# Token-wise convolution with expert routing: gate scores of two groups through the convolution, one softmax buffer, 128-row weight loads

## The chip, the cores and the metric

The kernel runs on one core of one Trainium2 chip. The metric is device time in microseconds (us) of one execution; three runs of the kernel before gave 272.96, 272.98 and 274.2 us, median 272.98.

## What is computed

```
w   = exp(weight_gen - max);  w = w / (sum over the 7 taps + 1e-9)        # (8, 4160, 8, 7)
out = einsum('bshk,bskhg->bshg', w, x_unf)     # x_unf: the token and the 6 before it, 8 heads x 24
...
scores  = einsum('bsd,d->bs', out, w_gate)                                # one score per token
for b in range(8):
    top_idx = argpartition(-scores[b], 128)[:128]
    xe = out[b, top_idx]
    ye = maximum(xe @ w1, 0) @ w2                                         # 192 -> 1024 -> 192
    out[b, top_idx] = xe + sigmoid(scores[b, top_idx])[:, None] * ye
```

x and weight_gen have 8 batches of 4160 tokens, in fp32. Every token has its own softmax weights over seven taps for each of 8 heads of 24 columns; then 128 tokens of each batch go through a small expert network.

## The kernel before, in words

**Tiling.** The 33280 tokens are cut into 278 windows of W = 120 tokens; a window takes 128 partitions (6 earlier tokens ahead of it). Four windows make a unit (U = 4), so there are 70 units, 0 to 69. The weights are handled in three groups of windows, GROUPS = ((0,80),(80,176),(176,278)), which are units 0 to 19, 20 to 43 and 44 to 69.

**Softmax.** Each group's weights are loaded in five chunks (`load_w`, 80, 96 or 102 rows of 5376 bytes) and handled with a window on a partition: `sm_exp` on ScalarE (L225), the sum over taps `sm_den` (VectorE L279 in group 0, GpSimd L283, L284, L287 in the others), the reciprocal as a logarithm and an exponential on ScalarE (L295, L297), `sm_start` (L267) and the product `sm_norm` (L309) on VectorE. The result stands in one of two buffers `amem`; `wt_head` transposes it on TensorE to `wt`, a token on a partition.

**Convolution.** Step si of a hand-written schedule does one piece of each of several units. GpSimd casts a unit of x to fp16 (`cast_x`, L164). VectorE multiplies wt with a mask (`band`, L766) into banded 128 x 128 matrices, one for each window and head: 128 x 3840 elements for a unit. For units in PBS, 50 to 65, one of the four windows is made on GpSimd, and VectorE's piece is 128 x 2880. `conv` is 32 matmuls (L792) with a band as weights and 24 columns of x. ScalarE copies the PSUM result (`evac`, L814) and SP stores it.

**Scores.** The score of a token is a sum over taps and heads of its softmax weight times the dot of an x row's head with the gate. The dots: `y_t` transposes x of a unit (L358, six matmuls), `y_x` copies xT out of PSUM (L369 on ScalarE, L367 on VectorE for every fifth unit), `y_d` (L381, L384, L387) multiplies it with the gate matrix gmat, and `y_e` (L392) keeps the dots in y16. When a group's dots are whole, `score_t` transposes them (L407), `score_x` copies them twice (Y0 and the same shifted by a token, L418, L419), `score_p` multiplies the softmax weights with them (L435, four pieces of 1920 elements), `score_m` sums over heads on TensorE (L451, four times eight matmuls), `score_r` adds the taps (L463) and `score_s`, `score_l` carry the scores through DRAM into the layout of the selection.

**Selection and experts.** After the last scores, candidates (L544 to L547), ranks (L588, L593, L600) and index lists (L606 to L628) follow on VectorE and TensorE. GpSimd then gathers 128 rows of each batch (`ex_gather`, L705), TensorE runs the two layers (L717, L730, L732, L740), VectorE adds (L742), and GpSimd scatters the rows back (`ex_scatter`, L747).

**What sets the order.** Each engine works through its own queue in the order in which the program issues. A step issues, in this order: moves due first (`pre`), loads and casts (`feed`), the band of unit si + 2, the copy and the store of unit si - 1, xT copies, moves due at its head (`first`), the convolution of unit si, the dots and transposes of later units, and the rest of its planned moves (`plan`):

```
        if si + 2 < NS and si >= 1:
            band(si + 2)
        if 1 <= si <= NS:
            evac(si - 1)
...
        if si < NS:
            conv(si)
        for j, u in enumerate(yd[si]):
            y_d(u, cts[si], j)
        for u in yt[si]:
            y_t(u)
        for mv in plan[si]:
            mv()
```

With Y_END = 47 the last dots are kept in step 49, where the scores of group 2 begin (`sc_moves`).

Of the kernel before, what the change touches and what calls it, by code (L numbers as in the profile page):

```python
# [18 lines left out]
P = 128  # L19
# [15 lines left out]
NV = 5  # L35

# [62 lines left out]
def fast_path(  # L99
# [11 lines left out]
    wrp = ctx.enter_context(tc.tile_pool(name="wrp", bufs=3))  # L111
# [3 lines left out]
    dtp = ctx.enter_context(tc.tile_pool(name="dtp", bufs=1))  # L115
    spp = ctx.enter_context(tc.tile_pool(name="spp", bufs=2))
# [9 lines left out]
    ps_m = ctx.enter_context(tc.tile_pool(name="ps_m", bufs=1, space=bass.MemoryType.PSUM))  # L126

# [62 lines left out]
    def load_w(gi, ci, home=None):  # L190
# [23 lines left out]
    def a_view(gi):  # L214
        return amem[gi % 2][:, 0:M * H * Q * 8].rearrange("p (c q k) -> p c q k", c=M * H, q=Q)
# [5 lines left out]

    def sm_exp(gi, ci):
        n, q0, q1, nq, col, cq = dims(gi, ci)
        wr = wraws.pop((gi, ci))
        nc.scalar.activation(  # L225
# [3 lines left out]
        )  # L229

# [72 lines left out]
    def sm_norm(gi, ci):  # L303
        n, q0, q1, nq, col, cq = dims(gi, ci)
        r2 = sm.pop((gi, ci))
        if gi and SE:
            sm_start(gi, ci, nc.vector)
        v = a_view(gi)[0:n, :, q0:q1, :].rearrange("p c q (k b) -> p c q k b", b=2)
        nc.vector.tensor_tensor(  # L309
# [3 lines left out]
        )  # L313
# [5 lines left out]
    def wt_t(gi, h):  # L319
# [4 lines left out]
        am = amem[gi % 2]  # L324
        tp = ps_t.tile([P, M, P], FP16, tag="tps", name="wtps")
# [22 lines left out]
    y16 = ypl.tile([P, NU * U, H], FP16, name="y16")  # L348
    ystate = {}

    def ntr(u):
        return nwin(u) * D // P

    def y_t(u):
        xf = xs[u].rearrange("p t d -> p (t d)")
        tp = ps_t.tile([P, M, P], FP16, tag="tps", name="xtps")
        for r in range(ntr(u)):
            nc.tensor.transpose(  # L358
                out=tp[:, r, :], in_=xf[:, r * P:(r + 1) * P], identity=ident16[:, :]
            )  # L360
        ystate[u] = tp

    def y_x(u, eng):
        tp = ystate.pop(u)
        xT = xtp.tile([P, NT, P], FP16, tag="xT", name="xT")
        if eng == "v":
            nc.vector.tensor_copy(out=xT[:, 0:ntr(u), :], in_=tp[:, 0:ntr(u), :])  # L367
        else:
            nc.scalar.copy(out=xT[:, 0:ntr(u), :], in_=tp[:, 0:ntr(u), :])  # L369
        ystate[u] = xT  # L370

    def y_d(u, cps, j):

        xT = ystate.pop(u)
        o = 2 * D + j * U * H
        yps = cps[:, 0, o:o + U * H].rearrange("p (w h) -> p w h", h=H)
        for r in range(ntr(u)):
            q, w = divmod(r, 3)
            lhs = xT[:, r, :]
            if w == 0:  # L380
                nc.tensor.matmul(out=yps[:, 2 * q, :], lhsT=lhs, rhs=gmat[:, 0, :],  # L381
                                 start=True, stop=False, skip_group_check=True)
            elif w == 1:
                nc.tensor.matmul(out=yps[:, 2 * q:2 * q + 2, :], lhsT=lhs, rhs=gmat[:, 1:3, :],  # L384
                                 start=False, stop=False, skip_group_check=True)
            else:
                nc.tensor.matmul(out=yps[:, 2 * q + 1, :], lhsT=lhs, rhs=gmat[:, 3, :],  # L387
                                 start=False, stop=True, skip_group_check=True)

    def y_e(us, cps):  # L390
        n = sum(nwin(u) for u in us)
        nc.scalar.copy(  # L392
            out=y16[:, us[0] * U:us[0] * U + n, :],
            in_=cps[:, 0, 2 * D:2 * D + n * H].rearrange("p (w h) -> p w h", h=H),
        )
# [890 lines left out]
```

## Time and profile before

| | |
|---|---|
| median of three runs | 272.98 us |
| the profiled execution's own time | 273.41 us |
| its span in the profile | 271.7 us |
| VectorE (DVE) busy | 225.9 us, 83% |
| TensorE (PE) / ScalarE (ACT) / GpSimd (POOL) busy | 169.4 / 169.6 / 163.5 us |
| moved by DMA | 63.74 MB |

The span runs from the first to the last recorded instruction; 273.41 - 271.7 = 1.7 us lie around it. The tables by stretch cut the span where the first band is made (28.4 us), where the last transposes of the dots start (178.3), where the scores are back from DRAM (199.6) and where the first gather can start (228.3). Busy time is that of instructions on an engine; a DMA share near 1 means that all 16 DMA engines had work nearly all the time.

### The profile page before, as it was taken

The page shows a single profiled execution, that of the slowest core. Times are in us where ns is not written, and L with a number is a line of the kernel's source. Part 1 is how long each engine was busy: PE and PEld are TensorE (multiplying, and loading weights), DVE is VectorE, ACT ScalarE, POOL GpSimd, SP SyncE. Part 2 cuts the span into 40 slices and gives each one's busy share as a digit, 9 for nine tenths or more (in the row PEclk, how much of TensorE's full clock was granted, in tenths as well). Part 3 has the DMA queues.
Part 4 walks back from the last instruction along what each step waited for, and adds up shares of the span by engine and source line. Part 5 has one row for each costly group of instructions (what it writes and reads, how often), then busy time and mean ns, then how long its engine had stood idle before and what let it go on. Part 6 is the DMA issues. An engine that isn't in the chain of part 4 may idle for free.

```text
span 271.7 us, 8756 instructions
## 1 busy us (share of the span) xinstructions
PE 169.4 (62%) x3605; PEld 157.1 (58%) x3605; DVE 225.9 (83%) x247; ACT 169.6 (62%) x331; POOL 163.5 (60%) x207
## 2 busy tenths in 40 slices
PE   0006577666787899466879697774833145499950
PEld 0006566656786899456778597774822134498740
DVE  4898999989999994998999868989989998495100
ACT  4763586889889367698797669561233922268620
POOL 8876596877337438989653623398346904863421
PEclk9999985556999656675589869655555555559965
DMA  7999999999999999989999969859446230746410
GB/s 173 248 296 271 272 274 253 292 312 317 345 343 324 309 316 330 320 260 326 340 352 358 353 180 251 281 161 203 89 116 189 62 109 17 234 127 185 131 45 22
DMA packets 77528, 63.74 MB, mean 235 GB/s; under 512 B 6488, under 2 KB 75648, under 8 KB 77483
## 3 DMA queue, kind: packets, MB, share of 16 engines
q1 hardware_dynamic: 75002, 60.76, 75.8%
q0 software_dynamic: 2032, 2.36, 3.9%
q8 instruction: 30, 0.49, 0.7%
q14 instruction: 16, 0.12, 0.1%
q10 hardware_dynamic: 448, 0.00, 0.1%
HBM read 37.41 MB, written 26.49 MB: 235 GB/s over the span
## 4 chain that ended last, share of the span: by engine, by line
DVE 29%; DMA 19%; issue 15%; PE 13%; POOL 12%; ACT 8%; SPq 1%; POOLq 1%; DVEq 0%; ACTq 0%
DMA xst<-in_x_dram 9%; DMA wraw<-in_weight_gen_dram 5%; DVE band__161 L766 5%; PE sps L451 4%; DVE band__162 L766 4%; ACT amem L225 3%; DVE band__163 L766 3%; DMA out_dram<-co 3%; DVE junk L593 3%; POOL s L283 3%; DVE amem L309 2%; DVE den L279 2%; PE cps L792 2%; POOL out_dram L747 2%; DVE sp L435 2%
## 5 line engine op out<-in xcount | busy, mean ns | idle before, releaser
L164 POOL CAST x<-xst 128x768 f16<-128x768 f32 x70 | 61.1, 887 | 46.4 <-DMA xst<-in_x_dram 30.5
L814 ACT COPY co<-cps 128x768 f32<-128x768 f32 x70 | 55.5, 797 | 32.4 <-PE cps L387 13.8
L358 PE MATMUL xtps<-ident,x 128*128 128x128 f16 x417 | 43.4, 268 | 11.6 <-DVE xT L367 6.1
L766 DVE TENSOR_TENSOR band__161<-wt,mask 128x3840 f16<-128x3840 f16 (+2 forms) x24 | 47.9, 1994 | 0.6 <-PE cps L792 0.5
L766 DVE TENSOR_TENSOR band__163<-wt,mask 128x3840 f16<-128x3840 f16 (+1 forms) x23 | 46.3, 2012 | 1.7 <-ACT wt L341 1.2
L766 DVE TENSOR_TENSOR band__162<-wt,mask 128x3840 f16<-128x3840 f16 (+1 forms) x23 | 46.8, 2033 | 0.2 <-PE cps L792 0.2
L369 ACT COPY xT<-xtps 128x768 f16<-128x768 f16 (+1 forms) x56 | 44.1, 817 | 2.2 <-PE xtps L358 2.2
L358 PEld LDWEIGHTS <-x 128*128 128x128 f16 x417 | 33.2, 121 | 12.8 <-POOL x L164 8.5
L792 PE MATMUL cps<-x,band__161 128*128 128x24 f16 x752 | 24.0, 179 | 10.4 <-DVE band__161 L766 8.9
L792 PEld LDWEIGHTS <-band__161 128*128 128x128 f16 x752 | 23.5, 103 | 11.5 <-DVE band__161 L766 9.5
L792 PEld LDWEIGHTS <-band__163 128*128 128x128 f16 x736 | 22.9, 102 | 9.5 <-issue 8.1
L792 PE MATMUL cps<-x,band__163 128*128 128x24 f16 x736 | 23.2, 178 | 8.1 <-ACT co L814 4.2
L792 PE MATMUL cps<-x,band__162 128*128 128x24 f16 x736 | 23.6, 179 | 3.5 <-DVE band__162 L766 2.2
L328 PE MATMUL wtps<-ident,amem 80*128 80x80 f16 (+2 forms) x192 | 13.1, 233 | 19.8 <-DVE amem L309 17.6
L792 PEld LDWEIGHTS <-band__162 128*128 128x128 f16 x736 | 22.9, 103 | 4.1 <-DVE band__162 L766 2.4
L451 PE MATMUL sps<-sp,ident 80*80 80x240 f16 (+2 forms) x96 | 18.1, 362 | 9.8 <-DVE sp L435 5.0
L328 PEld LDWEIGHTS <-amem 80*128 80x128 f16 (+2 forms) x192 | 11.6, 117 | 20.8 <-DVE amem L309 17.7
L381 PE MATMUL cps<-gmat,xT 128*128 128x8 f16 x139 | 15.5, 168 | 12.1 <-DVE xT L367 11.8
L225 ACT ACTIVATE amem<-wraw 96x1344 f16<-96x1344 f32 (+2 forms) x13 | 17.2, 1320 | 7.4 <-DVE sp L435 3.6
L451 PEld LDWEIGHTS <-ident 80*80 80x80 f16 (+2 forms) x96 | 15.4, 172 | 10.4 <-issue 6.7
L309 DVE TENSOR_TENSOR amem<-amem,r 80x1536 f16<-80x1536 f16 (+2 forms) x15 | 19.0, 1267 | 0.7 <-ACT r L297 0.2
L381 PEld LDWEIGHTS <-xT 128*128 128x128 f16 x139 | 11.9, 100 | 12.7 <-DVE xT L367 12.4
(177 smaller groups left out, 387.9 us busy)
## 6 DMA issues: line engine op xcount, KB each, us to landing
xst<-in_x_dram SPq DMA_DIRECT2D x68, 384.0 KB
out_dram<-co SPq DMA_DIRECT2D x69, 360.0 KB
wraw<-in_weight_gen_dram SPq DMA_DIRECT2D x10, 504.0 KB
wraw<-in_weight_gen_dram SPq DMA_DIRECT2D x3, 420.0 KB
amem<-in_weight_gen_dram SPq DMA_DIRECT2D x2, 420.0 KB
wea<-in_moe_w_dram POOLq DMA_DIRECT2D x1, 384.0 KB, 8.0
xst<-in_x_dram SPq DMA_DIRECT2D x1, 288.0 KB
wea<-in_moe_w_dram POOLq DMA_DIRECT2D x1, 256.0 KB, 6.7
```

Of the source, the lines that this page charges most:

```text
L164: nc.gpsimd.tensor_copy(out=t.rearrange("p u d -> p (u d)")[:, 0:n], in_=xst.pop(u).rearrange("p u d -> p (u d)")[:, 0:n],)
L225: nc.scalar.activation(out=a_view(gi)[0:n, :, q0:q1, 0:K].rearrange("p c q k -> p q c k"), in_=wr[0:n, 0:nq * M, :].rearrange("p (q m) (h ...
L283: nc.gpsimd.tensor_tensor(out=s4, in0=av[:, :, :, 0:4], in1=av[:, :, :, 4:8], op=ALU.add)
L309: nc.vector.tensor_tensor(out=v, in0=v, in1=r2[0:n, 0:cq, :].rearrange("p (c q) b -> p c q b", q=nq)[:, :, :, None, :] .to_broadcast([n, M ...
L328: nc.tensor.transpose(out=tp[:, m, 0:n], in_=am[0:n, o:o + P], identity=ident16[0:n, 0:n])
L358: nc.tensor.transpose(out=tp[:, r, :], in_=xf[:, r * P:(r + 1) * P], identity=ident16[:, :])
L369: nc.scalar.copy(out=xT[:, 0:ntr(u), :], in_=tp[:, 0:ntr(u), :])
L381: nc.tensor.matmul(out=yps[:, 2 * q, :], lhsT=lhs, rhs=gmat[:, 0, :], start=True, stop=False, skip_group_check=True)
L451: nc.tensor.matmul(out=sps[0:n].rearrange("p m q k -> p m (q k)"), lhsT=ident16[0:n, 0:n], rhs=sp[0:n, :, h, :], start=(h == 0), stop=(h = ...
L766: eng.tensor_tensor(out=bt[:, o:o + n * H * BC].rearrange("p (c q m) -> p c q m", q=NQ, m=M), in0=wts[gi][:, l:l + n].rearrange("p w h m - ...
L792: nc.tensor.matmul(out=cps[:, w // 2, (w % 2) * D + h * G:(w % 2) * D + (h + 1) * G], lhsT=bt[:, o:o + P], rhs=xwin(si * U + w)[:, h * G:( ...
L814: nc.scalar.copy(out=co.rearrange("p (j w) d -> p j (w d)", w=2)[:, 0:n], in_=cts[si][:, 0:n, 0:2 * D],)
```

## The change

- **Scores of groups 0 and 1 by the convolution.** A head of x becomes 25 columns (GY = 25) instead of 24: the cast writes runs of 24 into rows of 25, and `y_k` (ScalarE) puts the head's dot into the 25th. For units below 44 `conv` runs with 25 columns, so a score per head stands beside the result; `y_s` (ScalarE) copies it in fp32 for every step, and at a group's end `head_m` (eight fp32 matmuls against the identity) sums over heads and transposes, `head_x` copies and stores. `score_t`, `score_x`, `score_p`, `score_m` and `score_r` are gone for these two groups.
- **Transposes.** A unit of x has 800 columns now, seven transposes, xT of 896 columns. The gate matrix is built from a row by matmuls and selects (`gate_mats`). The dots of the first four units are made ahead of the loop (YP = 4); Y_END is 50, the last dots are kept in step 52.
- **Group 2** reads the transposed dots out of PSUM directly (no copies; the shifted ones come from a transpose with a turned identity); its four `score_p` stand in one step, its four sums in the next.
- **One softmax buffer.** `amem` is single, group 2's softmax moves from steps after group 0's scores to 17 to 32 (SM2), its transposes to 33 to 40 (WT2). One clearing of the second buffer (L866) is gone, and of group 0's sums over taps one goes to TensorE (seven matmuls).
- **Weight loads.** `wrp` has five buffers instead of three. Chunks of groups 0 and 1 are loaded with 128 rows instead of 80 and 96; all five of group 1 are issued ahead of the loop.
- **GpSimd** makes a quarter of the band for units 52 to 61 instead of 50 to 65. The order of gathers and scatters at the end differs.

The diff, cut:

```diff
+GY = G + 1
+DY = H * GY
-    wrp = ctx.enter_context(tc.tile_pool(name="wrp", bufs=3))
+    wrp = ctx.enter_context(tc.tile_pool(name="wrp", bufs=5))
...
+        if u < XR:
+            nc.gpsimd.memset(t[:, :, G], 0.0)
         nc.gpsimd.tensor_copy(
-            out=t.rearrange("p u d -> p (u d)")[:, 0:n],
-            in_=xst.pop(u).rearrange("p u d -> p (u d)")[:, 0:n],
+            out=t[:, 0:n, 0:G],
+            in_=xst.pop(u).rearrange("p u (h g) -> p (u h) g", g=G)[:, 0:n],
         )
...
-        cuts = [0, n // 16 * 16] + ([n] if n % 16 else [])
+        if n > 60 and w0 + P < TOT:
+            cuts = [0, P]
+        else:
+            cuts = [0, n // 16 * 16] + ([n] if n % 16 else [])
...
+    def y_k(u, yps):
+        n = nwin(u) * H
+        nc.scalar.copy(out=xs[u][:, 0:n, G], in_=yps.rearrange("p w h -> p (w h)")[:, 0:n])
...
+    def y_s(si):
...
+            nc.scalar.copy(
+                out=ysc[:, si * U:si * U + n, :].rearrange("p (j w) h -> p j (w h)", w=2),
+                in_=cts[si][:, 0:n // 2, 0:2 * DY].rearrange("p j (c g) -> p j c g", g=GY)[:, :, :, G],
+            )
...
+        nc_ = GY if si * U < GROUPS[2][0] else G
...
-                    out=cps[:, w // 2, (w % 2) * D + h * G:(w % 2) * D + (h + 1) * G],
-                    lhsT=bt[:, o:o + P], rhs=xwin(si * U + w)[:, h * G:(h + 1) * G],
+                    out=cps[:, w // 2, c:c + nc_],
+                    lhsT=bt[:, o:o + P], rhs=xwin(si * U + w)[:, h, 0:nc_],
...
-    LEND = 44
-    Y_END = 47
+    LEND = 46
+    Y_END = 50
-    PBS = range(50, 66)
+    PBS = range(52, 62)
-    SM2 = (0, 2, 4, 6, 8)
-    WT2 = (12, 13, 14, 15, 16, 17, 18, 19)
+    SM2 = (17, 20, 23, 26, 29)
+    LW2 = (8, 10, 13, 16, 19)
+    WT2 = (33, 34, 35, 36, 37, 38, 39, 40)
+    DP = "vvtvv"
...
-    pad(1)
-    feed(2)
-    load_w(1, 0)
...
+    for n, c in PF:
+        feed(n)
+        if c is not None:
+            load_w(1, c)
+    cast_to(YP)
```

**VectorE, where group 2's scores stand.** In the kernel before, the products (sp) stand in two pairs with a band (128x2880) between the pairs, and two more bands behind the first one of step 49:

```order
L367 COPY xT<-xtps 128x768
L766 TENSOR_TENSOR band__161<-wt_2931,mask 128x3840
L766 TENSOR_TENSOR band__162<-wt_2931,mask 128x3840
L766 TENSOR_TENSOR band__163<-wt_2931,mask 128x2880
L766 TENSOR_TENSOR band__161<-wt_2931,mask 128x2880
L435 TENSOR_TENSOR sp<-amem_128,Y_4047 102x1920
L435 TENSOR_TENSOR sp<-amem_128,Y_4048 102x1920
L766 TENSOR_TENSOR band__162<-wt_2931,mask 128x2880
L463 TENSOR_REDUCE sc<-sps 102x2x15 x2
```

In the changed kernel:

```order
L850 TENSOR_TENSOR band__157<-wt_3009,mask 128x3840
L415 COPY xT<-xtps 128x896
L850 TENSOR_TENSOR band__155<-wt_3009,mask 128x3840
L850 TENSOR_TENSOR band__156<-wt_3009,mask 128x2880
L850 TENSOR_TENSOR band__157<-wt_3009,mask 128x2880
L850 TENSOR_TENSOR band__155<-wt_3009,mask 128x2880
L518 TENSOR_TENSOR sp<-amem_126,ytps 102x1920 x4
L850 TENSOR_TENSOR band__156<-wt_3009,mask 128x2880
L546 TENSOR_REDUCE sc<-sps 102x2x15 x4
```

The sp stand behind the band of unit 54 (51 before), read ytps (PSUM) instead of Y, and are four in a row; one band lies between them and the four sums.

**GpSimd, ahead of the first casts of x.** Before:

```order
L539 CAST boffS<-bo 128x8
L677 MEMSET xe__155 128x192
...
L909 AFFINE_SELECT gsel<-wcol 128x8
L914 AFFINE_SELECT gmat<-gsel 128x8
...
L164 CAST x_314<-xst 128x768
L164 CAST x_318<-xst 128x768
```

In the changed kernel wcol comes from ScalarE behind seven matmuls that `gate_mats` issues after the fourth chunk of group 0's softmax:

```order
L1013 COPY grow<-grow 1x200 x3
L1027 AFFINE_SELECT gmat<-wcol 128x192
L1032 AFFINE_SELECT gmat<-gmat 128x192
L1027 AFFINE_SELECT gmat<-wcol 128x32
L1032 AFFINE_SELECT gmat<-gmat 128x32
L1037 AFFINE_SELECT gmat<-gmat 128x32
L171 MEMSET x_322 128x32
L172 CAST x_322<-xst 128x32x24
```

All casts now stand behind the selects that read wcol, and each of the first 24 has a memset of the 25th columns ahead of it.

**GpSimd, the last gathers and scatters.** Before; the rows of batch b's scatter end in a range of (b + 1) x 4160 rows:

```order
L747 DMA out_dram<-xm,sel_i 20800x192
L746 MEMSET tick 1x1
L747 DMA out_dram<-xm,sel_i 24960x192
L704 MEMSET tick 1x1
L705 DMA xm<-out_dram,sel_i 128x192
L746 MEMSET tick 1x1
L747 DMA out_dram<-xm,sel_i 29120x192
```

In the changed kernel:

```order
L831 DMA out_dram<-xe,sel_i 16640x192
L788 MEMSET tick 1x1
L789 DMA xe<-out_dram,sel_i 128x192
L830 MEMSET tick 1x1
L831 DMA out_dram<-xe,sel_i 20800x192
L830 MEMSET tick 1x1
L831 DMA out_dram<-xe,sel_i 24960x192
```

The last gather (batch 7) stood behind the scatter of batch 5 and stands behind that of batch 3 now.

## Rows read from the trace of the kernel before

**Rows 1.** Busy time by stretch: us, then each engine, granted PE clock, DMA share, GB/s.
```profile
0.00:28.40 28.40, 4.89 (x65) 4.41 (x65) 22.29 (x28) 16.41 (x32) 22.03 (x56) 1.00 0.97 251
28.40:178.30 149.90, 112.51 (x2643) 107.57 (x2643) 140.27 (x100) 115.57 (x219) 92.20 (x99) 0.73 1.00 304
178.30:199.60 21.30, 14.89 (x264) 14.38 (x264) 18.35 (x15) 7.31 (x9) 15.73 (x12) 0.50 0.64 135
199.60:228.30 28.70, 9.04 (x189) 7.12 (x186) 27.39 (x81) 11.45 (x29) 12.67 (x9) 0.50 0.36 106
228.30:271.70 43.40, 28.10 (x450) 23.59 (x449) 17.57 (x27) 18.84 (x43) 20.87 (x33) 0.70 0.41 119
```

**Rows 2.** Groups by line and shape, DVE, 28.4 to 178.3: count | busy, mean ns | idle before.
```profile
L766 DVE TENSOR_TENSOR band__161<-wt,mask 128x3840 f16<-128x3840 f16 x17 | 36.4, 2142 | 0.6 <-PE cps L792 0.5
...
L367 DVE COPY xT<-xtps 128x768 f16<-128x768 f16 x14 | 7.6, 544 | 0.0
...
L435 DVE TENSOR_TENSOR sp<-amem,Y 80x1920 f16<-80x1920 f16 x4 | 5.0, 1261 | 0.0
L435 DVE TENSOR_TENSOR sp<-amem,Y 96x1920 f16<-96x1920 f16 x4 | 4.6, 1142 | 0.0
...
L463 DVE TENSOR_REDUCE sc<-sps 96x30 f32<-96x210 f32 x4 | 1.5, 367 | 1.8 <-PE sps L451 1.8
```

**Rows 3.** The same view, ACT and POOL, 28.4 to 178.3.
```profile
L392 ACT CAST y<-cps 128x32 f16<-128x32 f32 x23 | 4.6, 199 | 0.0
...
L164 POOL CAST x<-xst 128x768 f16<-128x768 f32 x61 | 51.7, 862 | 42.4 <-DMA xst<-in_x_dram 26.6 <-PE cps L792 8.6 <-PE xtps L358 4.4
L284 POOL TENSOR_TENSOR s<-s 96x384 f32<-96x384 f32 x5 | 4.6, 918 | 0.4
...
L287 POOL TENSOR_TENSOR den<-s 96x192 f32<-96x192 f32 x5 | 4.4, 885 | 0.4
```

**Rows 4.** The chain of waits, 178 to 196: start, us, what.
```profile
178.28 1.77 PE ytps L407 x8
...
180.06 1.02 ACT Y L418
...
182.45 3.37 PE sps L451 x16
...
193.97 1.79 DMA sc_d<-sc
```

**Rows 5.** In order of time, POOL, PE and DVE at the end: start, us, what.
```profile
257.91 1.05 POOL L705 DMA_INDIRECT xm<-out_dram,sel_i  x1 [0.23 <-issue]
...
257.09 0.99 PE L740 MATMUL yeps<-wea,hT 128*128 128x192 bf16 x8 [0.30 <-issue]
...
263.68 1.61 PE L740 MATMUL yeps<-wea,hT 128*128 128x192 bf16 x8
...
265.34 0.42 DVE L742 SCALAR_TENSOR_TENSOR xm<-yeps,gates,xm 128x192 f32<-128x192 f32 x1 [6.80 <-PE yeps L740]
```

**Rows 6.** In order of time, DVE, then POOL's first cast, in the startup.
```profile
22.12 2.31 DVE L866 COPY amem<-zero 128x960 f16<-128x960 f16 x1
...
28.38 2.15 DVE L766 TENSOR_TENSOR band__161<-wt,mask 128x3840 f16<-128x3840 f16 x1
...
15.48 0.82 POOL L164 CAST x<-xst 128x768 f16<-128x768 f32 x1 [0.27 <-DMA xst<-in_x_dram]
```

**Rows 7.** In order of time, DVE, products and a band of group 2's scores.
```profile
181.11 2.35 DVE L435 TENSOR_TENSOR sp<-amem,Y 102x1920 f16<-102x1920 f16 x2 [0.84 <-ACT Y L418]
183.38 1.64 DVE L766 TENSOR_TENSOR band__162<-wt,mask 128x2880 f16<-128x2880 f16 x1
...
186.14 4.96 DVE L435 TENSOR_TENSOR sp<-amem,Y 102x1920 f16<-102x1920 f16 x2
```

**Rows 8.** Busy time by stretch, the first 10 us and 129 to 156.
```profile
0.00:10.00 10.00, 0.28 (x1) 0.10 (x1) 5.74 (x11) 5.13 (x9) 8.44 (x31) 1.00 0.83 195
129.00:156.00 27.00, 20.69 (x446) 20.07 (x447) 26.31 (x21) 20.82 (x37) 14.74 (x17) 0.82 1.07 351
```

More of the change, by code (lines that the diff above doesn't have):

```diff
@@ L220, in dims, with ins, apart @@
         return w1 - w0, q0, q1, q1 - q0, gi * NWC + ci, M * H * (q1 - q0)
+    def ins(i):
+        return i.ins if hasattr(i, "ins") else i
+    def apart(gi, ci, eng, i):
+        for c in range(NWC):
+            for e in "svtg":
+                if c != ci and e != eng:
+                    tc.declare_no_dep(ins(i), group=f"sm{gi}_{c}{e}",
+                                      reason="other chunks own other bytes")
+        tc.add_to_no_dep_group(f"sm{gi}_{ci}{eng}", ins(i))
     def sm_exp(gi, ci):
@@ L229, in sm_exp @@
         )
+        apart(gi, ci, "s", e)
     sm = {}
@@ L365, in y_x @@
         xT = xtp.tile([P, NT, P], FP16, tag="xT", name="xT")
[L366 to L369, printed above, removed]
+        ch = ych(u)
+        nf = sum(n == P for _, n, _ in ch)
+        parts = [(P, 0, nf)] + [(n, r, r + 1) for _, n, r in ch if n < P]
+        for n, u0, u1 in parts:
+            if eng == "v":
+                nc.vector.tensor_copy(out=xT[0:n, u0:u1, :], in_=tp[0:n, u0:u1, :])
+            else:
+                nc.scalar.copy(out=xT[0:n, u0:u1, :], in_=tp[0:n, u0:u1, :])
@@ L370, in y_x, with y_d @@
         ystate[u] = xT
-    def y_d(u, cps, j):
+    def y_d(u, yps):
         xT = ystate.pop(u)
[L375 to L388, printed above, removed]
@@ L390, in y_e @@
-    def y_e(us, cps):
[L391 to L395, printed above, removed]
-    NT = U * D // P
-    yts = {}
-    def score_t(gi):
+        ch = ych(u)
+        for i, (c, n, r) in enumerate(ch):
+            c0 = (NT - 1) * P if r == NT - 1 else c
+            a, b = c0 // DY, (c + n - 1) // DY + 1
+            nc.tensor.matmul(
+                out=yps[:, a:b, :], lhsT=xT[0:n, r, :], rhs=gmat[0:n, r, a:b, :],
+                start=(i == 0), stop=(i == len(ch) - 1), skip_group_check=True,
+            )
@@ L403, in score_t, with head_m, head_x @@
+    def head_m(gi):
         w0, w1 = GROUPS[gi]
         n = w1 - w0
-        tp = ps_t.tile([P, H, P], FP16, tag="tps", name="ytps")
+        hp = ps_t.tile([P, P], FP32, tag="tps", name="hps")
+        for h in range(H):
+            nc.tensor.matmul(
+                out=hp[0:n, :], lhsT=ysc[:, w0:w1, h], rhs=identity[:, :],
+                start=(h == 0), stop=(h == H - 1),
+            )
+        scs[gi] = hp
+    def head_x(gi):
+        w0, w1 = GROUPS[gi]
+        sc = smp.tile([P, W], FP32, tag="sc", name="sch")
+        nc.scalar.copy(out=sc[0:w1 - w0, :], in_=scs[gi][0:w1 - w0, 0:W])
+        nc.sync.dma_start(out=sc_d[w0:w1, :], in_=sc[0:w1 - w0, :])
@@ L698, in fast_path @@
     NXE = 8
-    xebuf = [consts.tile([CAP, D], FP32, name=f"xe{i}_") for i in range(4)]
+    xebuf = []
     xeTb = [consts.tile([P, 2, P], BF16, name=f"xeT{i}_") for i in range(2)]
@@ L941, in fast_path @@
+    yp4 = ps_t.tile([P, YP * U, H], FP32, tag="tps", name="yp4")
+    for u in range(YP):
+        y_d(u, yp4[:, u * U:(u + 1) * U, :])
+    for u in range(YP):
+        y_k(u, yp4[:, u * U:(u + 1) * U, :])
     NS = NU
@@ L973, in fast_path @@
     ydone = {}
-    for u in range(NU):
-        s = u * Y_END // NU
+    for u in range(YP, NU):
+        s = (u - YP) * Y_END // (NU - YP)
+        assert u * U >= GROUPS[2][0] or s + 3 <= u, u
         yt[s].append(u)
```

336 lines of the change are left out of this document (197 added, 139 removed).

## The prediction

> **What bounds the kernel now.** Start with the table by stretch [rows 1]. It shows five stages with different limits. Until 28.4 us the first softmax and transposes run and no band exists. From 28.4 to 178.3 VectorE is busy 140.27 of 149.9 us, more than any other engine; the DMA share is 1.00 at 304 GB/s. Then come a score chain (21.3 us) and a ranking on VectorE (27.39 of 28.7 us busy). The last 43.4 us are gathers, expert layers and scatters, in which no engine is busy for more than two thirds. Next, the groups by line in the long stage [rows 2]: a band takes 2.14 us and hardly waits; what stands between bands is the price of everything else on VectorE. Then the same groups on the other engines [rows 3]: GpSimd's casts wait 26.6 us for x, but also 8.6 and 4.4 us for a free x buffer, so x was at times as far ahead as its buffers allow. Last, the chain of waits through the scores [rows 4] and the order of time at the end [rows 5]: batch 7's gather starts at 257.91, and its second layer at 263.68, where batch 6's started at 257.09.
>
> I call T the start of group 2's transposes of dots: 178.28 before [rows 4]. The sum is made against the profiled execution's 273.41 us (span 271.7, 1.7 around it), 0.43 above the median of 272.98; I keep that difference as noise.
>
> **Startup: +0.5.** VectorE loses the clearing of the second buffer, 2.31 us [rows 6], and one sum over taps. That would be a gain of up to 3 us if VectorE were last here. But the casts of x, which began at 15.48 [rows 6], now stand on GpSimd behind selects that wait for ScalarE and for the softmax's fourth chunk, and 28 transposes of four units of x stand on TensorE ahead of the first transposes of the weights. I take the first band at 28.9 instead of 28.38. Bounds: -3 (the removed work counts in full), +4 (the four units' casts, 0.86 each, and their memsets in full).
>
> **First band to T: -4.6.** VectorE sets the pace. Removed: eight products of 1.26 and 1.14 us and eight sums of 0.37 [rows 2]. The start of a following instruction lies 0.08 us inside the one ahead (181.11 + 2.35 against 183.38 [rows 7]), so they occupy 8 x 1.12 + 8 x 0.29 = 11.3 us. Added: T moves three steps on, from band 50 to band 53 as the last ahead of it. Band 50 becomes a full one (+0.5), 51 is full (2.06), 52 and 53 are three-quarter bands (1.56 each, from 1.64 [rows 7]): +5.7. Thirteen xT copies are wider by a sixth, 0.544 / 6 each [rows 2]: at most +1.2, taken as 1.0. Sum -11.3 + 5.7 + 1.0 = -4.6. The shift of group 2's softmax keeps its VectorE work. What hides the rest: ScalarE gains 44 copies of a column (`y_s`), `y_k` and wider xT copies. The nearest row, a copy of 32 columns, is 0.199 us [rows 3]; 44 x 0.11 to 0.23 is 5 to 10 us, and with the rest some 12. It has 149.9 - 115.6 = 34 us free [rows 1], so nothing of it is taken onto the path; bounds 0 and +5 where it delays a band's buffer. GpSimd's cast writes runs of 24; I take 0.95 us from 0.86 [rows 3], since the runs are long, and bound it by the strided adds below. A 25th column in a matmul is taken as free: a twenty-fourth more columns in the convolutions, on an engine with 149.9 - 112.5 = 37 us free [rows 1]; were all its matmuls a twenty-fourth longer, 4.7 us of these would go. The head sums run on TensorE in its free time; nobody waits for their scores before the selection. Startup and this stage give T = 178.28 + 0.5 - 4.6 = 174.2.
>
> **DMA, from both sides.** Ten weight loads with 128 rows add 5 x 48 + 5 x 32 rows of 5376 bytes, 2.15 MB. Before, 28.4 x 0.251 + 149.9 x 0.304 = 52.7 MB had moved by T [rows 1]. With three more stores (1.1 MB) it is 55.9 MB by 174.2, of which 7.3 in the startup: 48.7 MB in 145.3 us, 335 GB/s. The stage reached 304 as a mean [rows 1] and 351 from 129 to 156 [rows 8], when no weights were loaded. The first 10 us, with loads of 80 rows, reached 195 at a share of 0.83 [rows 8]. So loads of few rows are slow per byte, and the extra rows cost something between nothing and 2.15 / 0.351 = 6.1 us of DMA time; I take it as hidden, as x had waited for buffers.
>
> [...] By bytes they cost 6.1 us, and if the DMA were the pace the sum would be 268. [...]
>
> **Score chain: -3.8.** Before: 21.3 us from T to the first candidate [rows 1]. Gone is ScalarE's copy of Y, 1.02 us [rows 4], and the second pair of products no longer waits behind a band and the first sums; that pair took 4.96 us while GpSimd's band pieces ran, against 2.35 for the first [rows 7]. Now four products run in a row. With a PSUM operand I take 1.15 each; bounds 1.14 [rows 2] and 2.48, half of 4.96 [rows 7]. A band of 1.64 us [rows 7] stands ahead of them at T, so they start at T + 2.0, when the first transposes (1.77 us [rows 4]) are done too, and end at T + 6.6. The four head sums (16 matmuls in 3.37 us, so 1.7 each [rows 4]) start at about T + 4.6, behind the second transposes and a convolution, and end at T + 11.4; the last reduce ends at T + 12. From the store of the scores at 193.97 [rows 4] to the candidates at 199.60 it was 5.6. Total 17.6, against 21.3: -3.8. [...]
>
> **Ranking: +1.5.** GpSimd's quarter bands end at unit 61 instead of 65, so three bands among the ranks are full: 3 x (2.06 - 1.56).
>
> **Experts: -5.0.** Batch 7's gather moves from behind batch 5's scatter to behind batch 3's, so its rows are there when TensorE is. Batches follow each other by 2.19 us in this phase (batch 6's second layer at 257.09 [rows 5]); batch 7's would start at 259.28 and take 0.99 as the others, instead of 263.68 and 1.61 [rows 5]: it ends at 260.3 instead of 265.3. What is late next is the last scatter, unchanged. Bounds: 0 if its rows come late again, -5.0.
>
> **Sum.** 0.5 - 4.6 - 3.8 + 1.5 - 5.0 = -11.4; 273.41 - 11.4 = 262.0 us.
>
> **Rivals.**
> *Forecast, 262 (257 to 266): 0.50.*
> *VectorE's idle time goes as well: 256.* In the long stage VectorE is idle for 9.6 us [rows 1]. With softmax chunks three steps apart and loads that finish earlier, some 5.6 us of it can vanish: 256.4. For it: the idle lies in waits for the softmax, not in bands [rows 2]. Against it: ScalarE gets fuller. 0.18. [...]
> *DMA sets T: 271 (268 to 275).* If the stage reaches 315 GB/s, between 304 and the 335 needed, T = 28.9 + 48.7 / 0.315 = 183.5, 9.3 later: 271. At 304 it would be 189, so 277. For it: a share of 1.00 already [rows 1]. Against it: casts that waited for free buffers [rows 3]. 0.20.
> *Slower: GpSimd's cast into rows of 25 sets the pace.* Its other work in the stage was 92.2 - 51.7 = 40.5 us [rows 1, 3], of which about 39 stay; from 19 us on, 66 casts of c each give T = 58 + 66c. That passes 174.2 at c = 1.76, and the whole is slower from c = 1.93. Rows that read or write short strided runs cost 918 / 384 = 2.4 ns an element and 885 / 192 = 4.6 [rows 3], which is c = 1.8 to 3.5; the plain cast costs 1.1. At c = 2.0 it is 278, at 2.2 it is 291. Against it: runs of 24 are far longer than the runs of 1 and 2 in those rows. 0.12.
>
> **How the numbers follow.** A measurement of this kernel can tell about 0.5% from no change, 1.4 us. Faster by more (below 271.6): 0.50 + 0.18 + 0.09 of the DMA case = 0.77. Within: 0.07 of the DMA case. Slower: 0.12 + 0.04 = 0.16. The range 253 to 272 leaves out the slow cast, the upper part of the DMA case and a little below: about 0.2.
>
> **What would show it.** Right: T near 174; casts below 1.2 us; bands that hardly wait; four products in a row at 1.1 to 1.3 us; 17 to 18 us from T to the candidates; batch 7's second layer 2.2 us behind batch 6's. Wrong: a first band beyond 31 us; casts near 1.8 us with bands waiting for GpSimd or for dots; a band stage at 304 GB/s with casts waiting for x throughout; products of over 2 us when read from PSUM; a gap ahead of the last batch.

## The result, and the profile after

The changed kernel takes 256.19 us (median of 4 runs, 255.51 to 258.05), against 272.97 for the kernel before beside it: a ratio of 0.939, 95% interval 0.933 to 0.945. The profiled execution took 255.91 us with a span of 254.2. The forecast was 262.0, range 253 to 272: the time lies inside, and the gain is 1.5 times the one forecast.

The table by stretch of the changed kernel, cut at the same events as [rows 1] (first band, T, candidates, first gather, end), only that the fourth cut is where the first gather starts:

```profile
0.00:29.04 29.04, 13.41 (x142) 10.78 (x142) 18.15 (x29) 18.88 (x36) 22.11 (x61) 0.97 0.81 278
29.04:176.06 147.02, 111.28 (x2776) 105.01 (x2775) 137.10 (x87) 125.05 (x279) 91.17 (x117) 0.77 1.04 327
176.06:190.84 14.78, 13.16 (x215) 12.86 (x212) 13.07 (x14) 4.52 (x6) 13.03 (x10) 0.71 0.82 151
190.84:219.95 29.11, 9.95 (x216) 7.99 (x217) 27.60 (x81) 11.90 (x32) 6.45 (x6) 0.51 0.36 107
219.95:254.20 34.25, 23.39 (x386) 19.87 (x385) 13.76 (x23) 17.07 (x41) 17.30 (x31) 0.80 0.45 129
```

Beside the forecast (before: first band at 28.38, T 178.28, candidates 199.60, first gather 228.61, end 271.7):

| stage | before | after | change | forecast |
|---|---|---|---|---|
| startup, to the first band | 28.4 | 29.0 | +0.7 | +0.5 |
| first band to T | 149.9 | 147.0 | -2.9 | -4.6 |
| T to candidates | 21.3 | 14.8 | -6.5 | -3.8 |
| candidates to first gather | 29.0 | 29.1 | +0.1 | +1.5 |
| first gather to the end | 43.1 | 34.3 | -8.8 | -5.0 |
| span | 271.7 | 254.2 | -17.5 | -11.4 |

The first two lines came as forecast: T fell at 174.07 and 174.04 in two kernels below that are the same up to there, so 176.06 is within what single executions differ; in this one TensorE shows a gap of 0.93 us right ahead of T in which it waited for nothing that the profile shows. The groups by line of that long stage answer to [rows 2, 3]; VectorE first, then ScalarE and GpSimd:

```profile
L850 DVE TENSOR_TENSOR band__156<-wt,mask 128x3840 f16<-128x3840 f16 x17 | 36.5, 2148 | 7.3 <-PE cps L878 7.3
L415 DVE COPY xT<-xtps 128x896 f16<-128x896 f16 x13 | 8.0, 618 | 0.0
```

```profile
L442 ACT CAST x<-cps 128x32 f16<-128x32 f32 x40 | 11.5, 351 | 0.0
L468 ACT COPY ysc<-cps 128x32 f32<-128x32 f32 x44 | 9.7, 221 | 0.0
...
L172 POOL CAST x<-xst 128x768 f16<-128x768 f32 x61 | 50.2, 833 | 40.7 <-DMA xst<-in_x_dram 31.3 <-PE xtps L404 5.0 <-PE cps L878 1.5
```

The cast into rows of 25 costs 0.833 us (0.862 before): the slower rival is out. What is new is 7.3 us in which bands wait for a convolution, in three pieces of up to 4.6 us; 4.6 and 2.4 of it stand behind the two head sums on TensorE. VectorE's idle time in this stage is as long as before (147.0 - 137.1 = 9.9 us against 9.6), but it is another one. In the kernel before, 5.0 us of it were waits for GpSimd's sums of the softmax and 1.8 us waits for sums of scores, and both are gone now:

```profile
DVE amem L267 <- POOL s L283: 5.0, 3, 3.1
DVE sc L463 <- PE sps L451: 1.8, 1, 1.8
```

The score chain answers to [rows 4, 7]; in order of time, TensorE, then VectorE:

```profile
176.06 1.73 PE L500 MATMUL ytps<-ident,y 128*102 128x128 f16 x8
177.59 1.70 PE L500 MATMUL ytps<-turn,y 128*102 128x128 f16 x8
179.08 1.06 PE L878 MATMUL cps<-x,band__157 128*128 128x24 f16 x32
179.97 5.70 PE L534 MATMUL sps<-sp,ident 102*102 102x240 f16 x32
...
177.83 4.35 DVE L518 TENSOR_TENSOR sp<-amem,ytps 102x1920 f16<-102x1920 f16 x4 [0.63 <-PE ytps L500]
```

Four products take 4.35 us, 1.09 each; 32 matmuls take 5.70, 0.178 each, against 0.211 before (3.37 / 16 [rows 4]). In the eight executions in which this stretch has the same order (this one, and those of the changed kernel's versions in experiments 1 to 5), T to the candidates took 14.6 to 17.3 us and the 32 matmuls 5.3 to 6.3, so 14.8 us is near the low end. The end answers to [rows 5]; the last gather stands at 240.78, ahead of four more scatters, and batch 7's second layer at 246.68; the scatters of batches 6 and 7 start at 246.21 and 248.41, 2.2 us apart:

```profile
240.78 1.04 POOL L789 DMA_INDIRECT xe<-out_dram,sel_i  x1 [0.23 <-issue]
```

```profile
246.68 0.99 PE L824 MATMUL yeps<-ew,hT 128*128 128x192 bf16 x8 [0.30 <-ACT hT L818]
```

### The profile page after: what moved, and what is told of

The parts are those of the page before. It is cut to its first block, busy times and chain, and to the rows that moved or that the text cites. A ratio compares the mean times of both kernels' runs of the same rounds, so it can differ in the third digit from the quotient of the medians.

```text
span 254.2 us, 9063 instructions
## 1 busy us (share of the span) xinstructions
PE 171.2 (67%) x3726; PEld 156.5 (62%) x3726; DVE 209.7 (82%) x231; ACT 177.4 (70%) x391; POOL 150.1 (59%) x222
## 3 DMA queue, kind: packets, MB, share of 16 engines
q0 software_dynamic: 2032, 2.36, 4.8%
## 4 chain that ended last, share of the span: by engine, by line
DVE 21%; PE 20%; issue 19%; DMA 14%; ACT 13%; POOL 9%; SPq 1%; POOLq 1%; DVEq 0%; ACTq 0%
DMA xst<-in_x_dram 10%; PE cps L878 4%; DVE band__156 L850 4%; ACT xT L417 4%; DVE band__155 L850 3%; DVE band__157 L850 3%; PE xtps L404 3%; ACT co L897 3%; PE hps L479 3%; DVE junk L676 3%; ACT amem L250 2%; PE sps L534 2%; POOL x L172 2%; DVE amem L348 2%; PE wtps L367 2%
## 5 line engine op out<-in xcount | busy, mean ns | idle before, releaser
L172 POOL CAST x<-xst 128x768 f16<-128x768 f32 x70 | 57.2, 828 | 42.8 <-DMA xst<-in_x_dram 33.4
L897 ACT COPY co<-cps 128x768 f32<-128x768 f32 x70 | 56.5, 810 | 27.6 <-PE cps L878 13.1
L417 ACT COPY xT<-xtps 128x896 f16<-128x896 f16 (+2 forms) x54 | 50.9, 968 | 0.3 <-PE xtps L404 0.3
L850 DVE TENSOR_TENSOR band__157<-wt,mask 128x3840 f16<-128x3840 f16 (+1 forms) x23 | 47.8, 2079 | 1.6 <-ACT wt L380 1.6
L404 PEld LDWEIGHTS <-x 128*128 128x128 f16 x487 | 36.3, 116 | 15.7 <-POOL x L172 13.7
L878 PE MATMUL cps<-x,band__156 128*128 128x25 f16 (+1 forms) x736 | 23.1, 177 | 10.4 <-ACT co L897 4.1
L878 PE MATMUL cps<-x,band__155 128*128 128x25 f16 (+1 forms) x752 | 24.1, 179 | 8.3 <-DVE band__155 L850 6.3
L878 PEld LDWEIGHTS <-band__156 128*128 128x128 f16 x736 | 22.2, 99 | 11.8 <-issue 8.2
L878 PEld LDWEIGHTS <-band__155 128*128 128x128 f16 x752 | 22.6, 101 | 9.3 <-DVE band__155 L850 7.0
L878 PE MATMUL cps<-x,band__157 128*128 128x25 f16 (+1 forms) x736 | 22.9, 178 | 6.7 <-DVE band__157 L850 6.3
L428 PE MATMUL cps<-gmat,xT 128*128 128x8 f16 (+1 forms) x459 | 19.6, 169 | 11.0 <-DVE xT L415 6.6
L878 PEld LDWEIGHTS <-band__157 128*128 128x128 f16 x736 | 21.8, 100 | 7.8 <-DVE band__157 L850 7.2
L428 PEld LDWEIGHTS <-xT 128*128 128x128 f16 x487 | 16.8, 99 | 11.7 <-DVE xT L415 7.0
L321 POOL TENSOR_TENSOR s<-amem 96x768 f32<-96x768 f16 (+1 forms) x10 | 16.6, 1660 | 10.8 <-ACT amem L250 10.8
L250 ACT ACTIVATE amem<-wraw 80x1344 f16<-80x1344 f32 (+2 forms) x15 | 20.2, 1344 | 0.2 <-DMA wraw<-in_weight_gen_dram 0.2
L348 DVE TENSOR_TENSOR amem<-amem,r 80x1536 f16<-80x1536 f16 (+2 forms) x15 | 16.4, 1100 | 0.9 <-ACT r L337 0.3
L380 ACT COPY wt<-wtps 128x816 f16<-128x816 f16 (+2 forms) x17 | 14.4, 875 | 0.9 <-PE wtps L367 0.9
```

What stands on the lines that cost most here:

```text
L172: nc.gpsimd.tensor_copy(out=t[:, 0:n, 0:G], in_=xst.pop(u).rearrange("p u (h g) -> p (u h) g", g=G)[:, 0:n],)
L250: e = nc.scalar.activation(out=a_view(gi)[0:n, :, q0:q1, 0:K].rearrange("p c q k -> p q c k"), in_=wr[0:n, 0:nq * M, :].rearrange("p (q m) ...
L321: apart(gi, ci, "g", nc.gpsimd.tensor_tensor(out=s4, in0=av[:, :, :, 0:4], in1=av[:, :, :, 4:8], op=ALU.add))
L348: apart(gi, ci, "v", nc.vector.tensor_tensor(out=v, in0=v, in1=r2[0:n, 0:cq, :].rearrange("p (c q) b -> p c q b", q=nq)[:, :, :, None, :] ...
L380: nc.scalar.copy(out=dst, in_=src)
L404: nc.tensor.transpose(out=tp[0:n, r, :], in_=xf[:, c:c + n], identity=ident16[:, :])
```

## The experiments

Ratios are to the kernel before on the same chip, with 95% intervals; the changed kernel's is 0.939 (0.933 to 0.945). The runs were made on several chips, on which the kernel before took 272.97 to 274.37 us, so compare two runs by their ratios rather than by their medians.

**1. Where the end's 8.8 us come from.** In the changed kernel, batch 7's gather two steps later:

```diff
-        g0 = max(s, blast[b] + 3, ya.get(b - NXE, 0) + 1)
+        g0 = max(s, blast[b] + 3 + (2 if b == 7 else 0), ya.get(b - NXE, 0) + 1)
```

> Batch 7's gather two steps later, behind batch 5's scatter as in the kernel before. Theory: the last batch waits for its rows again, so its second layer starts 6.5 us behind batch 6's (2.2 in the changed kernel) and the whole takes 256.2 + 5.0 = 261. Rival: the expert phase became shorter for another reason (fewer convolutions left in it), and batch 7's place is hidden: 256 to 257.

260.19 us, ratio 0.955 (0.950 to 0.960). From the first gather to the end it is 38.5 us, 4.2 more than in the changed kernel, and the last batch waits 2.73 us for its rows again:

```profile
247.47 0.30 PE L801 MATMUL xeTp<-identity,xe 128*128 128x128 f32 x1 [2.73 <-DMA xe<-out_dram,sel_i]
```

The theory holds. The same done alone in the kernel before (there `blast[b] + 1` for b = 7, `blast[b] + 3` for the others, and s0 kept at `blast[b] + 3` or later):

> The kernel before, with batch 7's gather alone moved two steps earlier, behind batch 3's scatter. Theory: that place alone is worth what the last batch waited, 4 to 5 us: 268 to 269 from 273.0. Rival: it shows only in the changed kernel, where the units end earlier against the gathers: 272 to 273.

270.99 us, ratio 0.990 (0.982 to 0.998), less gain than expected; the kernel before took 274.37 beside it. The stage falls from 43.1 to 38.8 us. The gather itself now waits 1.85 us for SP's queue (L91), and the place is worth 4.3 us in the stage, 3.4 in the time.

**2. GpSimd's band pieces at the end.** The rest of the 8.8 us was unforeseen. In the changed kernel, PBS up to 65 again:

```diff
-    PBS = range(52, 62)
+    PBS = range(52, 66)
```

> GpSimd makes a quarter of the band for units 62 to 65 again. Theory: those band pieces stand behind the gathers on GpSimd, the convolutions wait for them and the first expert layers wait behind these on TensorE, which was most of the long way from the first gather to the first scatter before (14.1 us against 10.5 now); VectorE gets 2.0 us less band work: from 256.2 to 258 to 260. Rival: that way became shorter because three fewer units were left after the selection; then VectorE's 2.0 us count alone: 254 to 256.

254.74 us, ratio 0.936 (0.929 to 0.942), no slower: the way from the first gather to the first scatter stays at 10.6 us. By this run the theory fell for the changed kernel. The selection ends two steps later there than in the kernel before, so the pieces of units 64 and 65 stand ahead of the gathers on GpSimd with this PBS too, and not behind the sixth gather as before. The last piece and the first gather, in order of time:

```profile
212.65 1.80 POOL L850 TENSOR_TENSOR band__157<-wt,mask_s 128x960 f16<-128x960 f16 x1 [6.61 <-PE cps L878]
...
217.76 1.13 POOL L789 DMA_INDIRECT ew<-out_dram,sel_i  x1 [3.23 <-DVE gates L711]
```

What the two pieces cost in the kernel before was tried there, with `PBS = range(50, 64)`:

> The kernel before, where GpSimd makes no quarter band for units 64 and 65, the two that stand behind its gathers. Theory: TensorE's convolutions and the first expert layer behind them waited for these pieces, so the way from the first gather to the first scatter falls from 14.1 us to 10.5 to 11.5 and the whole from 273.0 to 269.5 to 270.5. Rival: the way is long because three more units are left there; VectorE makes two more quarters (1.0 us): 273 to 274.

270.07 us, ratio 0.986 (0.977 to 0.995). The first scatter comes 10.5 us behind the first gather, as in the changed kernel; it was 14.1. In order of time on GpSimd, the kernel before and then this one:

```profile
236.30 1.81 POOL L766 TENSOR_TENSOR band__162<-wt,mask_s 128x960 f16<-128x960 f16 x1
238.06 1.82 POOL L766 TENSOR_TENSOR band__163<-wt,mask_s 128x960 f16<-128x960 f16 x1
...
242.75 1.02 POOL L747 DMA_INDIRECT out_dram<-xe__155,sel_i  x1 [1.55 <-DVE xe__155 L742]
```

```profile
229.17 1.13 POOL L705 DMA_INDIRECT xe__155<-out_dram,sel_i  x1 [3.23 <-DVE gates L628]
...
239.65 1.03 POOL L747 DMA_INDIRECT out_dram<-xe__155,sel_i  x1 [1.40 <-DVE xe__155 L742]
```

The two pieces ended at 238.1 and 239.9, the convolutions of units 64 and 65 could not start sooner, and behind the first of these on TensorE stands the first batch's second layer (L740). The wait shows best in experiment 1's version of the kernel before, which has the same two pieces:

```profile
237.55 0.41 PE L792 MATMUL cps<-x,band__162 128*128 128x24 f16 x9 [1.56 <-POOL band__162 L766]
```

Without the two pieces the stage is 3.9 us shorter (43.1 to 39.2). With the gather's 4.2 or 4.3 the two account for some 8.1 of the 8.8 us. The rival (fewer units left) fell: this kernel has as many left as before.

**3. Weight loads of 128 rows.** Undone in the changed kernel:

```diff
-        if n > 60 and w0 + P < TOT:
+        if False:
```

> Weight loads of groups 0 and 1 with 80 and 96 rows again, 2.15 MB less. By bytes (2.15 MB at 351 GB/s, 6.1 us of DMA time, half of it in the startup): 252 to 254 if the DMA sets the pace, 256 if it doesn't. If a load of few rows takes as long as one of 128: 256, and the first weight load lands no earlier. If few rows are slower, or the order of queues is worse: 257 to 260.

259.34 us, ratio 0.951 (0.946 to 0.956): 2.15 MB less, and 3.2 us slower. The table by stretch until 60 us, the changed kernel and this one:

```profile
0.00:10.00 10.00, 0.28 (x1) 0.17 (x2) 6.71 (x16) 6.25 (x10) 8.50 (x29) 1.00 0.81 311
0.00:29.00 29.00, 13.37 (x142) 10.78 (x142) 18.15 (x28) 18.87 (x36) 22.11 (x61) 0.98 0.81 278
29.00:60.00 31.00, 19.02 (x467) 17.24 (x465) 30.76 (x19) 26.77 (x65) 25.80 (x38) 0.67 1.04 344
```

```profile
0.00:10.00 10.00, 0.28 (x1) 0.17 (x2) 6.75 (x16) 6.21 (x10) 8.49 (x29) 1.00 0.83 203
0.00:29.00 29.00, 13.46 (x142) 10.85 (x142) 18.16 (x28) 18.74 (x36) 21.50 (x60) 0.98 0.83 218
29.00:60.00 31.00, 20.70 (x492) 19.03 (x490) 30.68 (x21) 26.97 (x64) 23.98 (x36) 0.61 1.03 303
```

In the first 10 us, which are mostly weight loads, 311 against 203 GB/s at nearly the same DMA share: a ratio of 1.53, where 128 to 80 rows is 1.6, so a load took about the same time with either. The softmax's second chunk, which waits for its load, also started at the same time, in the changed kernel and in this one:

```profile
6.65 1.33 ACT L250 ACTIVATE amem<-wraw 80x1344 f16<-80x1344 f32 x1 [0.17 <-DMA wraw<-in_weight_gen_dram]
6.61 1.33 ACT L250 ACTIVATE amem<-wraw 80x1344 f16<-80x1344 f32 x1 [0.24 <-DMA wraw<-in_weight_gen_dram]
```

By 60 us the changed kernel has moved 29 x 0.060 + 31 x 0.041 = 3.0 MB more, of which 2.15 are the extra rows; the other 0.86 MB are x and stores that are ahead. So in this kernel the extra rows cost nothing and few rows cost something on top; why they do more than break even stays open. The price by bytes (6.1 us) is refuted.

The other side, 128 rows alone in the kernel before (the same `cuts = [0, P]` for groups 0 and 1):

> The kernel before with weight loads of 128 rows for groups 0 and 1 alone. Theory: a load of few rows takes at least as long as one of 128, as the undone change showed (3.2 us slower with few rows): in this kernel VectorE has the more work and the DMA less weight, so 271 to 273 from 273 to 274. Rival by bytes: 2.15 MB more, 6 us of DMA time: 275 to 279.

273.33 us, ratio 1.000 (0.997 to 1.002), just above the 271 to 273 expected. The startup moves 314 GB/s instead of 250 in its first 29 us, but here the loads did land later. The second chunk's softmax started at 7.67, against 6.93 to 7.00 in three executions with 80 rows, and the first 10 us moved 253 GB/s against 195, a ratio of 1.3 and not 1.6:

```profile
7.67 1.33 ACT L227 ACTIVATE amem<-wraw 80x1344 f16<-80x1344 f32 x1 [0.37 <-DMA wraw<-in_weight_gen_dram]
```

The first band came at 29.1 (28.4 to 28.6 in the three) and T at 179.3 (178.3 before). So the whole shows no price and no gain. That VectorE is the pace there, which would explain the missing gain, is argued from [rows 1].

**4. What the head sums cost, and what stands behind them.** The eight fp32 matmuls spread over eight steps:

```diff
-            at(s + HM, head_m, gi)
-            at0(s + HM + 1, head_x, gi)
+            for i in range(H):
+                at(s + HM + i, head_m, gi, [i])
+            at0(s + HM + H, head_x, gi)
```

> The eight fp32 matmuls that sum over heads stand one in each of eight steps instead of eight in one step (their result shares a PSUM bank with the mask). Theory: in the changed kernel TensorE does them in one piece of 3.2 us and more, and VectorE's bands wait 4.6 and 2.4 us for the convolution behind it; spread, these 7 us go: 249 to 252. Rival: something else (x from the DMA, ScalarE) is only just behind and takes most of it: 254 to 256. Against both: bands that share a bank with the sums may wait for them: 257 or more.

264.14 us, ratio 0.965 (0.960 to 0.969), 8 us slower, by the third case: 13 bands wait, 13.6 us in all, for a sum that writes into the mask's tile.

```profile
DVE band__156 L851 <- PE mask L481: 6.4, 5, 2.1
DVE band__155 L851 <- PE mask L481: 5.5, 6, 1.8
DVE band__157 L851 <- PE mask L481: 1.7, 2, 0.9
```

This run says nothing on the sums themselves. The next does: a VectorE reduction over heads, then one transpose.

```diff
+        nc.vector.tensor_reduce(out=hsum[:, 0:w1 - w0], in_=ysc[:, w0:w1, :], axis=AX.X, op=ALU.add)
...
-        for h in range(H):
-            nc.tensor.matmul(
-                out=hp[0:n, :], lhsT=ysc[:, w0:w1, h], rhs=identity[:, :],
-                start=(h == 0), stop=(h == H - 1),
-            )
+        nc.tensor.transpose(out=hp[0:n, :], in_=hsum[:, 0:n], identity=identity[:, :])
```

> The sum over heads by one VectorE reduction of 640 or 768 elements for each of the two groups, then one fp32 transpose on TensorE in place of eight matmuls. Theory: VectorE's waits of 4.6 and 2.4 us behind the eight matmuls go, the reductions add 0.8 us each: 256.2 - 7.0 + 1.6 = 250.8 (249 to 253). Rival: the DMA is only just behind, x or a store buffer comes later and takes the gain: 254 to 256.5.

255.23 us, ratio 0.928 (0.919 to 0.938), in the rival's range. By the medians 1 us was gained, by the ratios 3, and the intervals of the two ratios overlap. The long waits are gone, but between 80 us and T VectorE still waits 2.7 us for convolutions (7.7 in the changed kernel):

```profile
DVE band__158 L851 <- PE cps L879: 1.0, 2, 0.8
DVE band__156 L851 <- PE cps L879: 0.9, 1, 0.9
DVE band__157 L851 <- PE cps L879: 0.8, 2, 0.6
```

The two reductions take 0.81 + 0.94 us of VectorE. So some 3 us were left to gain, and 1 to 3 came. In the same stretch, the waits of ScalarE's copy for a free store buffer grew from 3.8 us (5.1 and 5.3 in the first runs of experiments 1 and 2) to 9.3; the changed kernel, then this one:

```profile
ACT co L897 <- DMA out_dram<-co: 3.8, 5, 1.6
```

```profile
ACT co L898 <- DMA out_dram<-co: 9.3, 9, 2.8
```

That agrees with the rival, by which the stores are just behind; it was read from these waits and not tried by itself. With adds on GpSimd instead of the reduction:

> The same with three adds on GpSimd instead of VectorE's reduction, about 2 us for each group on an engine with time to spare. Theory: 249 to 251, up to 1.6 us below the reductions on VectorE. Rival: GpSimd stops its casts until the group's last convolution is copied, x comes late once and it is slower than the reductions: 253 to 256.

256.99 us, ratio 0.937 (0.928 to 0.945): no better than the changed kernel, as the rival had it, though above its 253 to 256.

**5. Is the DMA the pace?** The changed kernel with 2.36 MB of loads more (twelve half units of x into a tile of which nothing is used):

```diff
+        if u in TW:
+            nc.sync.dma_start(out=twice[:, :, :],
+                in_=ap_of(x_flat, x_flat.offset + row0(lo) * D, [[D, P], [W * D, 2], [1, D]]))
```

> The changed kernel with 12 more loads of half a unit of x (2.36 MB in all, at units 20, 22 to 42) into a tile that nobody reads. Theory: the DMA is about as tight as VectorE in the band stage (327 GB/s at a share of 1.04), so 2.36 / 0.327 = 7.2 us of DMA time show in T by 3 to 7 us: 259 to 263. Rival: VectorE and TensorE set the pace and the DMA has room: 256 to 257.

267.34 us, ratio 0.978 (0.973 to 0.982), above the 259 to 263 of the theory; T at 184.5, 8.4 us later than in the changed kernel and 10.5 later than in the first runs of experiments 1 and 2. From 29 to 60 us it moved 344 GB/s and then 317, 323 and 340 by stretches, the changed kernel 344, 322, 325 and 324: the rate did not rise to take the bytes, the stage grew. From 29 to 174 us both moved nearly the same, 47.6 to 47.8 MB, so the extra loads put others off. T comes later by more than the 7.2 us worked out; the profile also shows 12.5 us in which SP's queue waited to write the same tile again, so how much of the rest is bytes stays open. The run agrees with a stage in which the DMA has no room, but doesn't show it: the same loads into separate tiles, which would tell the two apart, were not run.

**6. A version that beats both.** The reduction over heads; group 2's sums ahead of the convolution of their step; quarter bands up to unit 64:

```diff
-    PBS = range(52, 62)
+    PBS = range(52, 65)
...
-            at(s + 1, score_m, gi, j)
-            at(s + 1, score_r, gi, j)
+            at0(s + 1, score_m, gi, j)
+            at0(s + 1, score_r, gi, j)
```

> The head sums by a VectorE reduction (as in the run before), the sums of group 2's scores ahead of the convolution of their step on TensorE, and GpSimd's quarter bands up to unit 64 (65's stood beside the one-hot matrices). Theory: -1 from the head sums, -1.5 to -2 from TensorE starting the sums when the first product is there, and -1.5 from three smaller bands among the ranks, with the one-hot matrices at 2.04 us: 251.5 to 253. Rival: what is gained up to T is taken by store buffers and DMA, and the scores come at the same time: 254 to 255.5.

253.67 us, ratio 0.926 (0.922 to 0.931), between the theory's range and the rival's. The ranking stage fell by 1.5 to 27.6 us as expected. The sums brought nothing: they start 3.2 us behind T (3.9 in the changed kernel), and take 6.80 us instead of 5.70:

```profile
176.72 6.80 PE L535 MATMUL sps<-sp,ident 102*102 102x240 f16 x32
```

That is 0.212 each, the price of [rows 4], where the granted clock was 0.50 [rows 1]; here it stayed at 0.50 throughout these matmuls. In the changed kernel a convolution ran ahead of the sums and the clock rose within them (0.50 from 176 to 184.5 us, 1.00 from 185.0 to their end at 185.7); that the convolution raised it is not shown. Then the candidates waited 1.8 us for scores from DRAM, so the load of the scores was put ahead of a store in SP's queue:

```diff
-        at(s + 2, score_l, gi)
+        atp(s + 2, score_l, gi)
```

> The combined kernel with the load of group 2's scores from DRAM ahead of the store of unit 53 in SP's queue. In the combined kernel the candidates waited 1.8 us for these scores, 6.8 us after the last reduce, where the changed kernel needed 4.7. Theory: that load stood behind a store that waits for the convolution now behind the sums; moved ahead of it, T to candidates falls from 17.2 to 15 to 15.5 and the whole from 253.7 to 251.5 to 252.5. Rival: the transfer itself is slow beside the x loads and stores: 253 to 254.

252.73 us, ratio 0.923 (0.919 to 0.927), 1.7% below the changed kernel by the ratios, whose intervals don't touch. T to candidates is 16.4 us: 0.8 better than the run before, not the 2 expected. The transfer itself took 2.96 us (3.67 in the run before it, 1.90 in the changed kernel), so the rival holds in part. The time lies between the two ranges here too.

## Why the prediction was right, and where it was off

- **Startup** (+0.5): +0.7, for the reason given; VectorE waits 4.9 us for the first transposed weights.
- **First band to T** (-4.6): -2.9, and -4.8 and -5.0 in two other executions of the same order. The work was priced about rightly: in the first run of experiment 1, where this stage fell by 4.8, VectorE is busy 135.3 us of it, against 140.27 before. What I costed at nothing, that the head sums on TensorE delay nobody, was wrong: 7.0 us of waits, which I had missed since I looked at who needs their result, and not at what is queued behind them. That the time came out near all the same is luck: about as many us of the old waits fell away (5.0 for the softmax, 1.8 for the scores), and the sum had neither.
- **DMA** (hidden): the extra rows cost nothing in the whole, in either kernel. The stage may be at the DMA's limit all the same, which I gave 0.20 as a case that sets T at 271; the rate was 327 GB/s, near the 335 that I had worked out as needed, and T was not late.
- **Score chain** (-3.8): -6.5. The start (first product 1.8 us behind T) and the product's 1.09 us are near the terms taken. The step that failed is the price of the sums, taken from [rows 4], 0.211 us a matmul at a granted clock of 0.50 [rows 1]: here the clock was 1.00 from 185.0 us on, and at 0.178 us a matmul the sums took 5.7 and not 6.8; they started 0.7 us sooner, and the way from the store to the candidates was 4.7 and not 5.6. Part of the -6.5 is chance: the other executions of this order give -4.0 to -6.7, and their 14.6 to 17.3 us reach the 17 to 18 that I named as a sign only at the upper end. The bound of 2.48, half of 4.96, was misread from [rows 7]: of those two products one took 1.15 us and the other 3.90.
- **Ranking** (+1.5): +0.1. The three full bands cost 1.5. I had missed what the missing GpSimd piece gives: beside it, twelve one-hot matrices took 3.43 us, without it 2.04. The kernel before, VectorE, then the piece on GpSimd:

```profile
220.19 2.04 DVE L606 TENSOR_SCALAR oh<-iota_f,rank 128x128 f16<-128x128 f16 x12
...
223.71 3.43 DVE L606 TENSOR_SCALAR oh<-iota_f,rank 128x128 f16<-128x128 f16 x12
...
223.49 1.80 POOL L766 TENSOR_TENSOR band__161<-wt,mask_s 128x960 f16<-128x960 f16 x1 [6.61 <-PE cps L792]
```

  With quarter bands to unit 65 in the changed kernel it is 3.44 again, to 64 it is not, and the stage is 27.6.
- **Experts** (-5.0): -8.8. The gather's place was mis-sized by little (4.2 and 4.3 in two runs). The step that failed is the bound "0 if its rows come late again, -5.0": it took the gather for the only thing that changes there. Two band pieces stood behind the sixth gather and cost 3.9 us, and in the changed kernel no piece stands there. The change of PBS, which I priced only among the ranks, would do this, but it isn't needed: with PBS up to 65 the pieces stand ahead of the gathers too (experiment 2), since the selection comes two steps later.
- **The rival at 256** gave the measured time for another reason: the waits for the softmax did go, 5.0 us, but the waits behind the head sums came in their place, and VectorE's idle time in the long stage did not shrink (9.9 us against 9.6).

So the sign and the main terms were right, the bands did not "hardly wait" as I had named for a sign, and four things were missed. Three helped: the GpSimd pieces beside VectorE, those ahead of TensorE, and the clock that rises within the sums. One cost time: the waits behind the head sums. That single terms came out near is in part luck.

## What to carry to other kernels

When a quarter of a job is given to another engine, look at every place where those pieces run: what is queued behind them there (here two pieces cost 3.9 us at the end of the kernel before), and what runs beside them on the engine that was to be relieved (twelve one-hot matrices took 3.43 us beside a piece, 2.04 without). A matmul group "that nobody waits for" can hold up what is queued behind it on TensorE: here bands waited 4.6 and 2.4 us for convolutions behind the two head sums. And before a wait is taken away, take off what the new work costs and ask which buffer comes free next: here 7 us of waits, less 1.75 us of reductions, gave 1 to 3 us.

## What the runs showed of the hardware that was not expected

- In the changed kernel a load of 128 rows of 5376 bytes took no longer than one of 80: 311 against 203 GB/s in the first 10 us, and the second chunk's softmax at 6.65 and 6.61. In the kernel before it did land later, 7.67 against 6.93 to 7.00.
- Of four VectorE products of two SBUF tensors, the one that ran beside two of GpSimd's band pieces took 3.90 us, the others 1.15 to 1.28. The four products of the kernel before, shortest, median and longest in ns:

```profile
L435 DVE TENSOR_TENSOR sp<-amem,Y x4: 1145/1215/3895, 181.1 to 190.0; 102x1920 f16<-102x1920 f16 x4
```

  The long one began at 186.14, within two pieces that GpSimd ran from 185.38 to 189.01, and ended about 1.0 us behind them. With one operand in PSUM the products took 1.09 each with such a piece beside them nearly all the time (177.72 to 184.86 on GpSimd). That the PSUM operand is what makes the difference was read from these rows and not tried by itself.
- 32 matmuls moved ahead of a convolution, 0.7 us nearer to T, took 6.80 us in two runs, with the granted clock at 0.50 throughout; behind the convolution they took 5.3 to 6.3 in eight executions, and in the changed kernel's profile the clock was 1.00 for the last 0.7 us of them.
